# One strided sum for pooled values, a new order of the first loads, two joined chunks and a moved wait

## The chip, the cores and the metric

One core of a Trainium2 chip runs the whole program. The metric is the device time of one execution in microseconds (us). The engines are TensorE (PE in profile rows; PEld is its weight load), VectorE (DVE), ScalarE (ACT), GpSimd (POOL) and SyncE (SP, which issues most DMAs). Each runs its own instruction stream in order, and they wait for one another through semaphores.

## The reference, cut to what matters

An attention layer with pooled keys and values feeds a mixture of experts in which each token takes one expert.

```python
# 8 batches, 8 heads, 576 positions, 64 wide; pool = 8, so 72 pooled keys per head
k_p = k.reshape(B, H, Sp, pool, D).mean(axis=3)
v_p = v.reshape(B, H, Sp, pool, D).mean(axis=3)
attn = softmax(q @ k_p^T / sqrt(D))
x = (attn @ v_p)                      # as rows: 4608 tokens x 512
e_idx = argmax(x @ w_gate, axis=1)    # one of 8 experts per token
out[mask_e] = gate_w * eom * (relu(x @ w1[e]) @ w2[e])   # 512 -> 1024 -> 512
```

## The kernel before, in words

**Attention and routing** (up to about 150 us) goes over 36 tiles of 128 tokens; a batch is 4.5 tiles. Each tile has two halves `a` (heads 0 to 2 or so, and the rest), and the loop at the end of `attention_and_routing` writes out the order by hand: for tile `i` it issues the scores on TensorE, the row maxima (`peak`, VectorE, line 281), the exponentials (`softmax`, ScalarE), and, for older tiles, the transposes of the probabilities, the product with the values (`values`) and the division by the sum (`normalise`, VectorE, line 332, after a reciprocal, line 326). Other work is put between these: `at(step, f, ...)` calls `f` after a given half tile, and a queue of generators gives out pieces through `work(n)`, four pieces per half tile. All engines take their instructions in this written order, so an instruction that waits holds back all that is written behind it on its engine.

**Pooling.** Keys and values are loaded unpooled, eight rows to a pooled row. For batches 1 to 7 GpSimd adds keys in halves (`pool_k`, line 201) and makes the first halving of the values (`halve_v`, line 223, five chunks of 256 columns); VectorE makes the other two halvings (`pool_v`, line 227), for three chunks and then for two, as four queue pieces from `pooled(b)`. For batch 0 VectorE does everything: `ready_k(0)` and `first_v(0)` are written before the loop, `ready_k(1)` and `first_v(1)` after the first half tile, ahead of the second half's `peak`. The buffer of unpooled values, `vt`, is one for all batches: the next batch's load waits until it has been pooled.

**First loads.** SyncE issues, in this order: keys of the first four heads' half (576 KB), all values (1280 KB), the first tile's queries (256 KB), the other keys (576 KB), the other queries (896 KB).

**Tail.** `TAIL` is an order written out by hand for the end of routing and the start of the first expert's work: `M` is one of eight chunks of the first layer on TensorE (12 matmuls of 384 columns, four of them on the low part of the tokens), `H` and `L` round it to a high and a low part on ScalarE and VectorE, `a d A D` split weights into high and low parts, `W` gives out routing pieces, `T` loads the table of jobs into registers, and `Y` is a chunk of the second layer. After it every engine changes over to its own loop over the experts' jobs.

**Experts** (from about 175 us): TensorE alternates the first layer (line 1015) and the second (line 996); VectorE scales the result (line 1186) and GpSimd scatters it to the output by an indirect DMA (line 1328). At the end of each job GpSimd waits until its scatters have landed, and at the very end for its last gathers.

Of the kernel before, what the change touches and what calls it, by code (L numbers as in the profile page):

```python
# [15 lines left out]
AF = mybir.ActivationFunctionType  # L16
# [7 lines left out]
P = 128  # L24
# [33 lines left out]

TAIL = 'M W9 a H L W3 d M a H L W6 d M a H L W6 d M a H L W6 d A M H L W12 A D M H L A D R M H L A D T M D Y Y Y Y Y H L'.split()
F0 = TAIL.count('Y')

AHEAD = {3: 8, 2: 8, 1: 2}
# [26 lines left out]
def attention_and_routing(ctx, tc, sh, qT, kT, v, wg, wst, xs):  # L91
# [95 lines left out]
    def load_v(b):  # L187
        nc.sync.dma_start(vt, v[b].rearrange("p (c f) -> p c f", c=5))

    def load_first():  # L190
        k_t[0], q_t[0] = sh.k[0], sh.q[0]
        k, q = kT[0].rearrange("p (c r n) -> p c r n", r=POOL, c=4), qT[0].rearrange("p (c s) -> p c s", c=4)
        nc.sync.dma_start(k_t[0][:, 0:2], k[:, 0:2])
        load_v(0)
        nc.sync.dma_start(q_t[0][:, :, 0:P], q[:, :, 0:P])
        nc.sync.dma_start(k_t[0][:, 2:4], k[:, 2:4])
        nc.sync.dma_start(q_t[0][:, :, P:S], q[:, :, P:S])

    def pool_k(b, eng, w, c0, c1):
        k = k_t[b][:, c0:c1]  # L200
        eng.tensor_tensor(k[:, :, 0:w], k[:, :, 0:w], k[:, :, w:2 * w], op=ALU.add)  # L201

    def scale_k(b, c0=0, c1=4):
        for h in range(2):
            r = slice(64 * h, 64 * h + 64)
            nc.scalar.activation(kbd[b % 2][r, c0:c1, KEYS * h:KEYS * h + KEYS], k_t[b][r, c0:c1, 0], AF.Copy, scale=1.0 / 64)

    def ready_k(a):
        for w in (4, 2, 1):
            pool_k(0, nc.vector, w, 2 * a, 2 * a + 2)  # L210
        scale_k(0, 2 * a, 2 * a + 2)

    def pooled_rows(b):
# [9 lines left out]
            nc.gpsimd.tensor_tensor(vt[:, c, 0:256], vt[:, c, 0:256], vt[:, c, 256:512], op=ALU.add)  # L223

    def pool_v(b, a, n):
        to = vt[:, part_v(a), 0:n] if n > D else pooled_rows(b)[:, part_v(a)]
        nc.vector.tensor_tensor(to, vt[:, part_v(a), 0:n], vt[:, part_v(a), n:2 * n], op=ALU.add)

    def first_v(a):
        for n in (4 * D, 2 * D, D):  # L230
            pool_v(0, a, n)

    def place_v(b, c):
        t = vbd[b % 2]
# [36 lines left out]
    def scores(i, a):  # L271
        s = s_t[i, a] = sh.p_h[(2 * i + a) % 3]
        for c in range(2):
            for r0, n, b, s0 in segments(i):
                nc.tensor.matmul(s[r0:r0 + n, 144 * c:144 * c + 144], q_t[b][:, 2 * a + c, s0:s0 + n],  # L275
                                 kbd[b % 2][:, 2 * a + c, :], start=True, stop=True)

    def peak(i, a):
# [208 lines left out]

    def first_layer(kind):
        if kind == "M":
            f = len(layered)  # L490
            layered.append((sh.p_h + sh.p_y[1:])[f % 4][:, 0:WIDE * P])
            hidden_chunk(nc, sh, f, layered[f], f == 0)
        elif kind == "Y":
            outputs.append(output_chunk(nc, sh, len(outputs), sh.p_y[0], 0))
        elif kind == "a":
            split_hi(halves[0])
        elif kind == "d":
            split_lo(halves.pop(0))
        elif kind == "A":
            split_piece.append(len(split_piece))  # L500
            split_hi(2 * 4 + split_piece[-1], 1)
        elif kind == "D":
            split_lo(2 * 4 + split_done.pop(), 1)
        elif kind == "T":
            assert not queue
            for eng in (nc.tensor, nc.scalar, nc.vector, nc.gpsimd, nc.sync):
                sh.loaded[eng.engine] = nc.values_load_multi_w_load_instructions(
                    sh.table[0:1, 0:E + 2], [eng.engine], min_val=0, max_val=1023,
                    skip_runtime_bounds_check_because="counts of a few bits each")[1]
        elif kind == "R":  # L510
# [16 lines left out]

    def pooled(b):
        for a in range(2):
            for n in (2 * D, D):  # L530
                pool_v(b, a, n)
                yield 0

    tick = [0]

# [48 lines left out]
    prepare_buffers(2)  # L584
    prepare_counts()
    ready_k(0)
    first_v(0)
    at(-0.5, ready_k, 1)
    at(-0.5, first_v, 1)
    at(1.5, prepare_routing)  # L590
    at(3, no_rows, E)
    for e in range(E):
# [57 lines left out]
    return x.rearrange("p g f -> p (g f)"), x.rearrange("p g (d t) -> p d g t", d=4), halves  # L650


def hidden_chunk(nc, sh, f, acc, late):
    terms = [(d, part, x) for d in range(4) for part, x in ((0, 0), (0, 1), (1, 0))]
    if late:
        terms.sort(key=lambda term: term[2])
    for d, part, x in terms:
        o = DM * f + P * d
        i = nc.tensor.matmul(acc, sh.w1[0][:, part, o:o + P], sh.xt[:, x, d, :], start=((d, part, x) == terms[0]), stop=((d, part, x) == terms[-1]))
    return i  # L660


def output_chunk(nc, sh, f, acc, k):
# [64 lines left out]
def experts(st, nc, sh, wst, xs, out):  # L728
# [557 lines left out]
    @blk.gpsimd  # L1286
    def _(eng):
        copy = nc.gpsimd.tensor_copy

        def columns(u):  # L1290
            u = nc.s_assert_within(u, 0, R - WIDE, skip_runtime_bounds_check_because="there are at most 50 slots")
            return ids[:, bass.ds(u, WIDE)]

        def past(name, val):
            val = eng.to_reg(val)
            eng.wait_ge(q["on"], 1)
            eng.wait_ge(q[name], val)

        def take(u):
            copy(nx, xm[:, :, ID - DM:ID - DM + 2]).then_inc(q["c"], 1)  # L1300
            copy(src, columns(u)).then_inc(q["c"], 1)  # L1301

        def gather(sems):
            for k in range(WIDE):
                nc.gpsimd.indirect_dma_start(out=xm[:, k].bitcast(I32), out_offset=None, in_=xs,  # L1305
                                             in_offset=bass.IndirectOffsetOnAxis(ap=src[:, k:k + 1], axis=0)).then_inc(sems[k], 16)

        def ahead(u, job, more):
            if not isinstance(job, int):
                for k in range(WIDE):  # L1310
                    past(f"x{k}", 16 * job - 16)
            with eng.If(more > 0):
                take(u + 3)
            with eng.If(more <= 0):
                take(u + 2)
            past("c", 3 * job + 1)
            gather(X)

        def body(e, size, job, u, single, nth, more, last, late):
            past("y", u + 1)  # L1320
            copy(sc[:, 0:3:4 - size], nx[:, 0:size, 1]).then_inc(q["sc"], 1)
            copy(dst, nx[:, :, 0]).then_inc(q["c"], 1)
            past("sc", job + 1)
            past("c", 3 * job + 5)
            ahead(u + size, job + 2, more)
            for k in range(size):
                past("y", u + k + 2)
                nc.gpsimd.indirect_dma_start(out=out, out_offset=bass.IndirectOffsetOnAxis(ap=dst[:, k:k + 1], axis=0),  # L1328
                                             in_=yb[2 if k == size - 1 else k], in_offset=None, bounds_check=N - 1, oob_is_err=False).then_inc(q["out"], 16)
            past("out", 16 * (u + size))  # L1330

        eng.nop().then_inc(q["on"], 1)
        rows = table(eng)
        with eng.If(rows[E + 1] > 2):
            eng.nop().then_inc(q["c"], 2)
        with eng.If(rows[E + 1] <= 2):
            copy(src, columns(0)).then_inc(q["c"], 2)
            past("c", 2)
            gather([q["g"]] * WIDE)
            past("g", 16 * WIDE)  # L1340
        ahead(0, 1, rows[E + 1] & 1)
        eng.wait_ge(q["t"], ROWS)
        job, slot = loops(eng, rows, body)
        for k in range(WIDE):
            past(f"x{k}", 16 * job + 16)


def program():
# [54 lines left out]
def layout(q, k, v, moe_w_gate, moe_w_output_gate, moe_w1, moe_w2):  # L1403
# [2 lines left out]
    wg = np.zeros((2, D, 11, GATE), np.float32)  # L1406
    for a, slot, head in ((0, 0, 0), (0, 1, 1), (1, 2, 3), (1, 3, 4), (0, 4, 1), (0, 5, 2), (1, 6, 6), (1, 7, 7), (0, 8, 4), (0, 9, 5), (0, 10, 6)):
        wg[a, :, slot] = gates[head]
    rows = v.reshape(B, H, KEYS, POOL * D)
    vs = np.zeros((B, P, 5, POOL * D), np.float32)  # L1410
    for chunk, r0, head, k0, n in VROWS:
        vs[:, r0:r0 + n, chunk] = rows[:, head, k0:k0 + n]
    return {
        "qT": c(q.reshape(B, 4, 2, S, D).transpose(0, 2, 4, 1, 3)).reshape(B, P, 4 * S),
        "kT": c(k.reshape(B, 4, 2, KEYS, POOL, D).transpose(0, 2, 5, 1, 4, 3)).reshape(B, P, 4 * POOL * KEYS),
        "v": vs.reshape(B, P, 5 * POOL * D),
        "wg": wg.reshape(P, 11 * GATE),
# [10 lines left out]
```

## Time and profile before

| | us |
|---|---|
| median of 3 runs | 607.02 |
| lowest and highest of them | 606.26, 607.34 |
| the profiled execution's own time | 603.94 |
| its span, first to last instruction | 602.1 |
| TensorE busy in the span | 572.3 (95%) |
| VectorE busy | 365.1 (61%) |
| ScalarE busy | 257.8 (43%) |
| GpSimd busy | 223.1 (37%) |

The granted TensorE clock was 0.998 of full speed. Shares of busy time are means over two very different stages: attention up to about 150 us, the experts from about 175 us on. Instructions of one engine can overlap a little in the rows, so that busy times are slightly too high, those of TensorE above all.

### The profile page before, as it was taken

The numbers are of one execution on the slowest core, as the hardware profiler recorded it, in microseconds if no ns is written. First come the engines' busy times: TensorE is split into PE (matmuls) and PEld (weight loads), VectorE is DVE, ScalarE is ACT, GpSimd is POOL, SyncE is SP. The second block draws the span as 40 slices with busy tenths as digits, with TensorE's granted clock in tenths as the row PEclk, the third lists the DMA queues.
The fourth block names the chain that finished last, engine by engine and source line by source line (L and its number), as shares of the span: only waits on it lengthen the run. The fifth ranks groups of instructions, "written<-read, shape, count | busy, mean of one in ns | idle before, by whom it ended". The sixth has DMA issues, their size and how long they took to land.

```text
span 602.1 us, 11826 instructions
## 1 busy us (share of the span) xinstructions
PE 572.3 (95%) x3427; PEld 519.2 (86%) x3428; DVE 365.1 (61%) x892; ACT 257.8 (43%) x709; POOL 223.1 (37%) x331
## 2 busy tenths in 40 slices
PE   2999999999899999999999999999999999999996
PEld 2898898888888989898989898898988898989894
DVE  6789999988888625698575323664263842232323
ACT  2988998787435304266344120441141420302120
POOL 2858789642524322233234131231202421213131
PEclk9999999999999999999999999999999999999999
DMA  9856899966377433589666213463033212010111
GB/s 337 312 236 270 316 349 369 348 232 198 140 238 182 170 99 118 147 234 335 177 215 201 62 37 88 139 195 65 35 139 102 46 21 84 2 52 19 41 30 36
DMA packets 44684, 96.61 MB, mean 160 GB/s; under 512 B 5515, under 2 KB 28475, under 8 KB 41664
## 3 DMA queue, kind: packets, MB, share of 16 engines
q1 hardware_dynamic: 29328, 48.95, 25.3%
q10 hardware_dynamic: 7488, 27.27, 13.5%
q0 software_dynamic: 7792, 19.61, 9.3%
q14 instruction: 57, 0.47, 0.3%
q8 instruction: 19, 0.31, 0.2%
HBM read 76.36 MB, written 22.91 MB: 165 GB/s over the span
## 4 chain that ended last, share of the span: by engine, by line
PE 68%; issue 2%; DVEq 0%; DVE 0%; POOL 0%; POOLq 0%
PE p_h L1015 34%; PE p_y L996 33%; PE p_y L665 1%; POOL out L1328 0%; DVE rows L1186 0%; DVEq L1189 0%; PE p_y L1050 0%; DVE q_even L1212 0%; DVEq L779 0%; DVEq L780 0%; DVEq L1219 0%; DVEq L910 0%; DVEq L837 0%; DVEq L1211 0%; DVEq L860 0%
## 5 line engine op out<-in xcount | busy, mean ns | idle before, releaser
L1095 ACT ACTIVATE ht<-p_h 128x384 fp32r<-128x384 f32 (+1 forms) x104 | 46.9, 451 | 245.9 <-PE p_h L1015 243.7
L1015 PE MATMUL p_h<-xt,w1b 128*128 128x384 f32 (+1 forms) x736 | 115.5, 317 | 1.9 <-issue 1.3
L1015 PEld LDWEIGHTS p_h<-xt,w1b 128*128 128x128 f32 x736 | 114.4, 189 | 3.2 <-issue 2.8
L1328 POOL DMA_INDIRECT out<-rows,dst x41 | 43.1, 1051 | 199.8 <-DVE rows L1186 196.6
L1197 DVE SCALAR_TENSOR_TENSOR ht<-p_h,ht 128x384 fp32r<-128x384 f32 (+1 forms) x104 | 52.3, 504 | 98.4 <-ACT ht L1095 98.3
L996 PE MATMUL p_y<-w2b,ht 128*128 128x512 f32 x480 | 110.4, 390 | 0.0
L996 PEld LDWEIGHTS p_y<-w2b,ht 128*128 128x128 f32 x480 | 89.8, 188 | 18.4
L1015 PE MATMUL p_h<-xt,w1a 128*128 128x256 f32 (+1 forms) x640 | 93.7, 306 | 1.2 <-DVE q_even L1212 1.0
L1015 PEld LDWEIGHTS p_h<-xt,w1a 128*128 128x128 f32 x640 | 92.8, 190 | 2.3 <-DVE q_even L1212 1.2
L996 PE MATMUL p_y<-w2a,ht 128*128 128x512 f32 x408 | 94.2, 390 | 0.4 <-PE p_y L665 0.4
L996 PEld LDWEIGHTS p_y<-w2a,ht 128*128 128x128 f32 x408 | 76.2, 188 | 16.4 <-issue 0.9
L1186 DVE TENSOR_SCALAR rows<-p_y,sc 128x512 f32<-128x512 f32 x41 | 30.1, 741 | 85.9 <-PE p_y L996 71.5
L287 ACT ACTIVATE p<-p_h,m 128x72 f32<-128x72 f32 x288 | 69.9, 345 | 13.4 <-DVE m L281 13.0
L309 PE MATMUL p_y<-vbd,pT 128*128 128x162 f32 (+3 forms) x400 | 68.5, 320 | 3.8 <-DVE xg L332 2.6
L1305 POOL DMA_INDIRECT rows<-xs,src x51 | 56.0, 1099 | 24.9 <-POOL src L1301 13.4
L309 PEld LDWEIGHTS p_y<-vbd,pT 128*128 128x128 f32 (+1 forms) x400 | 54.2, 179 | 8.7 <-issue 2.5
L440 POOL DMA_INDIRECT xs<-xg,where x36 | 36.1, 1003 | 42.5 <-DVE grec L326 20.7
L201 POOL TENSOR_TENSOR kq<-kq 128x288 f32<-128x288 f32 (+1 forms) x63 | 40.8, 673 | 15.0 <-DMA kq<-kT 14.2
L275 PE MATMUL p_h<-kbd,q_even 128*128 128x144 f32 (+1 forms) x160 | 28.9, 308 | 11.6 <-DMA q_even<-qT 8.8
L332 DVE TENSOR_TENSOR xg<-p_y,grec 128x240 f32<-128x240 f32 x72 | 35.3, 490 | 1.3
L1150 DVE STREAM_TRANSPOSE turned<-rows 128x512 f32<-128x512 f32 x51 | 32.4, 686 | 4.0 <-DMA rows<-xs 2.2
L275 PEld LDWEIGHTS p_h<-kbd,q_even 128*128 128x128 f32 (+1 forms) x160 | 22.9, 191 | 13.7 <-issue 9.3
(170 smaller groups left out, 660.3 us busy)
## 6 DMA issues: line engine op xcount, KB each, us to landing
stage<-wst ACTq DMA_DIRECT2D x52, 512.0 KB, 4.7
rows<-v SPq DMA_DIRECT2D x8, 1280.0 KB, 6.3
kq<-kT SPq DMA_DIRECT2D x7, 1152.0 KB, 12.0
rows<-xs SPq DMA_DIRECT2D x36, 192.0 KB, 3.8
stage<-wst SPq DMA_DIRECT2D x12, 512.0 KB, 6.0
kq<-qT SPq DMA_DIRECT2D x4, 1152.0 KB, 9.5
q_even<-qT SPq DMA_DIRECT2D x3, 1152.0 KB, 8.8
rows<-xs SPq DMA_DIRECT2D x20, 128.0 KB
```

What stands on the lines that cost most here:

```text
L201: eng.tensor_tensor(k[:, :, 0:w], k[:, :, 0:w], k[:, :, w:2 * w], op=ALU.add)
L275: nc.tensor.matmul(s[r0:r0 + n, 144 * c:144 * c + 144], q_t[b][:, 2 * a + c, s0:s0 + n], kbd[b % 2][:, 2 * a + c, :], start=True, stop=True)
L287: nc.scalar.activation(pt[i % 3][:, o:o + KEYS], sv[:, h], AF.Exp, bias=m[:, h:h + 1])
L309: nc.tensor.matmul(av[r0:r0 + n, COLS * h:COLS * (h + n_heads)], pT[:, c, r0:r0 + n], vbd[b % 2][:, slot:slot + n_heads].rearrange("p h f ...
L332: nc.vector.tensor_tensor(xg[g][:, j, 0:LEAD + DM].rearrange("p (f h) -> p f h", h=H)[:, :, hs], avv[:, :, 0:GATE + D].rearrange("p h f -> ...
L440: ins = nc.gpsimd.indirect_dma_start(out=whole_rows(xs), out_offset=bass.IndirectOffsetOnAxis(ap=where, axis=0), in_=x.bitcast(I32), in_of ...
L996: i = mm(to, ht[:, h, f, P * k:P * k + P], w[:, part, o:o + DM], start=(f == 0 and part == 0 and h == 0), stop=(f == 7 and h == 1))
L1015: i = mm(to, w[:, part, o:o + P], x, start=(d == 0 and k == 0), stop=(d == 3 and k == len(terms) - 1))
L1095: act(ht[:, 0, f, 0:size * P], p_h[f % DEEP][:, 0:size * P], AF.Relu).then_inc(q["hh"], 1)
L1197: nc.vector.scalar_tensor_tensor(ht[:, 1, f, 0:n], src, 0.0, ht[:, 0, f, 0:n].bitcast(F32), op0=ALU.max, op1=ALU.subtract).then_inc(q["hl" ...
L1305: nc.gpsimd.indirect_dma_start(out=xm[:, k].bitcast(I32), out_offset=None, in_=xs, in_offset=bass.IndirectOffsetOnAxis(ap=src[:, k:k + 1], ...
L1328: nc.gpsimd.indirect_dma_start(out=out, out_offset=bass.IndirectOffsetOnAxis(ap=dst[:, k:k + 1], axis=0), in_=yb[2 if k == size - 1 else k ...
```

## The change

Four parts. VectorE's pooling becomes one `tensor_reduce` over a rearranged view, so that the summed index is innermost, with a step of 64 numbers (values) or 72 (the first batch's keys): 1536 and 1024 inputs per partition for batch 0's values, 768 and 512 for each later batch, 1152 for each half of batch 0's keys. Both reductions of batch 0's values are written after `ready_k(1)`, still ahead of the second half's `peak`; for later batches `pooled(b)` has two pieces instead of four. The first loads go in the order keys, queries, keys, queries, values, with batch 0's queries laid out so that each load has whole rows. In `TAIL` the first `M` computes chunks 0 and 1 together, the high part's matmuls of both before the low part's, and the other `M`s each move up by one place. GpSimd's wait for a job's scatters moves to the beginning of the next job, the last one behind the waits for the last gathers; the bound of the scatter's index sits in one register.

```diff
-TAIL = 'M W9 a H L W3 d M a H L W6 d M a H L W6 d M a H L W6 d A M H L W12 A D M H L A D R M H L A D T M D Y Y Y Y Y H L'.split()
+TAIL = 'M W9 a H L W3 d M a H L W6 d M a H L W6 d M a H L W6 d M A H L W12 A D M H L A D R M H L A D T D Y Y Y Y Y H L'.split()
...
     def load_first():
         k_t[0], q_t[0] = sh.k[0], sh.q[0]
-        k, q = kT[0].rearrange("p (c r n) -> p c r n", r=POOL, c=4), qT[0].rearrange("p (c s) -> p c s", c=4)
+        k = kT[0].rearrange("p (c r n) -> p c r n", r=POOL, c=4)
+        q0 = q_t[0].rearrange("p c s -> p (c s)")
         nc.sync.dma_start(k_t[0][:, 0:2], k[:, 0:2])
+        nc.sync.dma_start(q0[:, 0:4 * P], qT[0][:, 0:4 * P])
+        nc.sync.dma_start(k_t[0][:, 2:4], k[:, 2:4])
+        nc.sync.dma_start(q0[:, 4 * P:], qT[0][:, 4 * P:])
         load_v(0)
-        nc.sync.dma_start(q_t[0][:, :, 0:P], q[:, :, 0:P])
-        nc.sync.dma_start(k_t[0][:, 2:4], k[:, 2:4])
-        nc.sync.dma_start(q_t[0][:, :, P:S], q[:, :, P:S])
...
+    first_keys = sh.stage[0][:, 0:4 * KEYS].rearrange("p (c n) -> p c n", c=4)
...
     def ready_k(a):
-        for w in (4, 2, 1):
-            pool_k(0, nc.vector, w, 2 * a, 2 * a + 2)
+        c = slice(2 * a, 2 * a + 2)
+        nc.vector.tensor_reduce(first_keys[:, c], k_t[0][:, c].rearrange("p c r n -> p c n r"), axis=AX.X, op=ALU.add)
         scale_k(0, 2 * a, 2 * a + 2)
...
     def pool_v(b, a, n):
-        to = vt[:, part_v(a), 0:n] if n > D else pooled_rows(b)[:, part_v(a)]
-        nc.vector.tensor_tensor(to, vt[:, part_v(a), 0:n], vt[:, part_v(a), n:2 * n], op=ALU.add)
-
-    def first_v(a):
-        for n in (4 * D, 2 * D, D):
-            pool_v(0, a, n)
+        nc.vector.tensor_reduce(pooled_rows(b)[:, part_v(a)],
+                                vt[:, part_v(a), 0:n * D].rearrange("p c (r d) -> p c d r", r=n), axis=AX.X, op=ALU.add)
...
         if kind == "M":
-            f = len(layered)
-            layered.append((sh.p_h + sh.p_y[1:])[f % 4][:, 0:WIDE * P])
-            hidden_chunk(nc, sh, f, layered[f], f == 0)
+            accs = {}
+            for _ in range(1 if layered else 2):
+                f = len(layered)
+                accs[f] = (sh.p_h + sh.p_y[1:])[f % 4][:, 0:WIDE * P]
+                layered.append(accs[f])
+            hidden_chunks(nc, sh, accs)
...
     def pooled(b):
         for a in range(2):
-            for n in (2 * D, D):
-                pool_v(b, a, n)
-                yield 0
+            pool_v(b, a, POOL // 2)
+            yield 0
...
     ready_k(0)
-    first_v(0)
     at(-0.5, ready_k, 1)
-    at(-0.5, first_v, 1)
+    for a in range(2):
+        at(-0.5, pool_v, 0, a, POOL)
...
         def body(e, size, job, u, single, nth, more, last, late):
+            with eng.If(job > 0):
+                past("out", 16 * u)
             past("y", u + 1)
...
-            past("out", 16 * (u + size))
-
+        limit = eng.to_reg(N - 1)
...
         for k in range(WIDE):
             past(f"x{k}", 16 * job + 16)
+        past("out", 16 * slot)
```

`hidden_chunks` issues the same 12 matmuls per chunk as `hidden_chunk` did, sorted so that the high part's come first over both chunks. `scale_k` reads batch 0's pooled keys from `first_keys`, and `queries` finds batch 0's queries in their new layout.

## Rows read from the trace of the kernel before

**Rows 1.** The chain that ended last, in order of time: start us, us, what.
```profile
175.23 7.77 PE p_y L665 x33
...
598.09 1.00 POOL out L1328
```

**Rows 2.** Busy time by stretch: stretch, its us, busy us (instructions) of each engine, clock, DMA.
```profile
40.00:60.00 20.00, 19.27 (x155) 17.94 (x154) 18.17 (x67) 16.70 (x69) 14.17 (x19) 1.00 0.64 240
...
250.00:400.00 150.00, 149.84 (x866) 137.13 (x865) 91.83 (x134) 60.21 (x98) 44.24 (x56) 1.00 0.54 164
```

**Rows 3.** VectorE's timeline in a tile without pooling; brackets: idle before, and what ended it.
```profile
48.34 0.19 DVE L326 RECIPROCAL grec<-p_y 128x5 f32<-128x5 f32 x1 [0.77 <-PE p_y L309]
```

**Rows 4.** VectorE's groups from 21 to 150 us: busy us, mean ns | idle.
```profile
L227 DVE TENSOR_TENSOR rows<-rows 128x384 f32<-128x384 f32 x7 | 6.8, 976 | 1.7 <-POOL rows L223 1.7
...
L227 DVE TENSOR_TENSOR vp<-rows 128x192 f32<-128x192 f32 x7 | 3.8, 544 | 0.2
...
L227 DVE TENSOR_TENSOR rows<-rows 128x256 f32<-128x256 f32 x7 | 3.2, 464 | 0.0
...
L227 DVE TENSOR_TENSOR vp<-rows 128x128 f32<-128x128 f32 x7 | 2.1, 297 | 0.0
```

**Rows 5.** Single lines of VectorE: ns minimum/median/maximum, first and last start, shapes.
```profile
L687 DVE TENSOR_REDUCE rows<-rows x2: 328/913/1498, 169.8 to 177.8; 128x12 f32<-128x84 f32 x1, 128x100 f32<-128x700 f32 x1
...
L348 DVE TENSOR_REDUCE lg<-xg x9: 671/676/678, 35.9 to 153.9; 128x64 f32<-128x512 f32 x9
...
L360 DVE TENSOR_REDUCE best<-cand x9: 168/170/186, 37.7 to 155.3; 128x4 f32<-128x32 f32 x9
...
L354 DVE TENSOR_TENSOR d<-lg,mx x9: 181/245/1699, 36.8 to 154.9; 128x32 f32<-128x32 f32 x9
```

**Rows 6.** DMA issues by line: count, KB each, median us to landing.
```profile
rows<-v SPq DMA_DIRECT2D x8, 1280.0 KB, 6.3
...
kq<-kT SPq DMA_DIRECT2D x2, 576.0 KB, 5.7
...
q_even<-qT SPq DMA_DIRECT2D x1, 896.0 KB, 9.3
...
q_even<-qT SPq DMA_DIRECT2D x1, 256.0 KB, 7.0
```

**Rows 7.** The timeline of the first 27 us, all engines.
```profile
4.64 1.60 DVE L201 TENSOR_TENSOR kq<-kq 128x576 f32<-128x576 f32 x3 [0.47 <-DMA kq<-kT]
...
6.33 0.65 ACT L206 ACTIVATE kbd<-kq 64x144 f32<-64x144 f32 x2 [4.05 <-DVE kq L201]
...
7.86 1.55 DVE L227 TENSOR_TENSOR rows<-rows 128x768 f32<-128x768 f32 x2 [1.62 <-DMA rows<-v]
...
8.82 1.30 PE L275 MATMUL p_h<-kbd,q_even 128*128 128x144 f32 x4 [8.82 <-DMA q_even<-qT]
...
14.22 0.46 DVE L281 TENSOR_REDUCE m<-p_h 128x4 f32<-128x288 f32 x1 [0.71 <-PE p_h L275]
...
14.71 1.92 ACT L287 ACTIVATE p<-p_h,m 128x72 f32<-128x72 f32 x8 [1.91 <-DVE m L281]
...
23.41 1.07 DVE L227 TENSOR_TENSOR rows<-rows 128x384 f32<-128x384 f32 x1 [1.03 <-POOL rows L223]
```

**Rows 8.** The timeline from 150 to 176 us, all engines.
```profile
154.08 0.97 PE L659 MATMUL p_h<-xt,w1a 128*128 128x384 f32 x4 [0.61 <-DVE xt L483]
...
157.41 0.56 DVE L520 SCALAR_TENSOR_TENSOR ht<-p_h,ht 128x384 fp32r<-128x384 f32 x1 [1.14 <-ACT ht L516]
...
173.64 0.55 DVE L520 SCALAR_TENSOR_TENSOR ht<-p_y,ht 128x384 fp32r<-128x384 f32 x1
```

**Rows 9.** The last scatter of outputs and GpSimd's queue after it, from 585 us.
```profile
DMA to landing us min/median/max: 2.8/2.8/2.8
...
L1295 POOLq FUSED_REGOPS  x2: 161/178/196, 601.1 to 601.3; - x2
...
L1297 POOLq EVENT_SEMAPHORE  x5: 17/17/42, 591.9 to 601.7; - x5
```

More of the change, by code (lines that the diff above doesn't have):

```diff
@@ L191, in load_first, with queries @@
         k_t[0], q_t[0] = sh.k[0], sh.q[0]
-        k, q = kT[0].rearrange("p (c r n) -> p c r n", r=POOL, c=4), qT[0].rearrange("p (c s) -> p c s", c=4)
+        k = kT[0].rearrange("p (c r n) -> p c r n", r=POOL, c=4)
+        q0 = q_t[0].rearrange("p c s -> p (c s)")
         nc.sync.dma_start(k_t[0][:, 0:2], k[:, 0:2])
+        nc.sync.dma_start(q0[:, 0:4 * P], qT[0][:, 0:4 * P])
+        nc.sync.dma_start(k_t[0][:, 2:4], k[:, 2:4])
+        nc.sync.dma_start(q0[:, 4 * P:], qT[0][:, 4 * P:])
         load_v(0)
-        nc.sync.dma_start(q_t[0][:, :, 0:P], q[:, :, 0:P])
-        nc.sync.dma_start(k_t[0][:, 2:4], k[:, 2:4])
-        nc.sync.dma_start(q_t[0][:, :, P:S], q[:, :, P:S])
+    def queries(b, c, s0, n):
+        if b:
+            return q_t[b][:, c, s0:s0 + n]
+        q0 = q_t[0].rearrange("p c s -> p (c s)")
+        o, w, s = (0, P, 0) if s0 < P else (4 * P, S - P, P)
+        o += w * c + s0 - s
+        return q0[:, o:o + n]
     def pool_k(b, eng, w, c0, c1):
@@ L205, in scale_k @@
             r = slice(64 * h, 64 * h + 64)
-            nc.scalar.activation(kbd[b % 2][r, c0:c1, KEYS * h:KEYS * h + KEYS], k_t[b][r, c0:c1, 0], AF.Copy, scale=1.0 / 64)
+            pooled = k_t[b][r, c0:c1, 0] if b else first_keys[r, c0:c1]
+            nc.scalar.activation(kbd[b % 2][r, c0:c1, KEYS * h:KEYS * h + KEYS], pooled, AF.Copy, scale=1.0 / 64)
     def ready_k(a):
-        for w in (4, 2, 1):
-            pool_k(0, nc.vector, w, 2 * a, 2 * a + 2)
+        c = slice(2 * a, 2 * a + 2)
+        nc.vector.tensor_reduce(first_keys[:, c], k_t[0][:, c].rearrange("p c r n -> p c n r"), axis=AX.X, op=ALU.add)
         scale_k(0, 2 * a, 2 * a + 2)
@@ L274, in scores @@
             for r0, n, b, s0 in segments(i):
-                nc.tensor.matmul(s[r0:r0 + n, 144 * c:144 * c + 144], q_t[b][:, 2 * a + c, s0:s0 + n],
+                nc.tensor.matmul(s[r0:r0 + n, 144 * c:144 * c + 144], queries(b, 2 * a + c, s0, n),
                                  kbd[b % 2][:, 2 * a + c, :], start=True, stop=True)
@@ L650, in turned_rows, with hidden_chunks @@
     return x.rearrange("p g f -> p (g f)"), x.rearrange("p g (d t) -> p d g t", d=4), halves
[L653 to L657, printed above, removed]
+def hidden_chunks(nc, sh, accs):
+    terms = [(f, d, part, x) for f in accs for d in range(4) for part, x in ((0, 0), (0, 1), (1, 0))]
+    if 0 in accs:
+        terms.sort(key=lambda term: term[3])
+    seen = {f: 0 for f in accs}
+    for f, d, part, x in terms:
         o = DM * f + P * d
-        i = nc.tensor.matmul(acc, sh.w1[0][:, part, o:o + P], sh.xt[:, x, d, :], start=((d, part, x) == terms[0]), stop=((d, part, x) == terms[-1]))
-    return i
+        nc.tensor.matmul(accs[f], sh.w1[0][:, part, o:o + P], sh.xt[:, x, d, :], start=(seen[f] == 0), stop=(seen[f] == 11))
+        seen[f] += 1
 def output_chunk(nc, sh, f, acc, k):
@@ L1328, in body @@
                 nc.gpsimd.indirect_dma_start(out=out, out_offset=bass.IndirectOffsetOnAxis(ap=dst[:, k:k + 1], axis=0),
-                                             in_=yb[2 if k == size - 1 else k], in_offset=None, bounds_check=N - 1, oob_is_err=False).then_inc(q["out"], 16)
-            past("out", 16 * (u + size))
+                                             in_=yb[2 if k == size - 1 else k], in_offset=None, bounds_check=limit, oob_is_err=False).then_inc(q["out"], 16)
+        limit = eng.to_reg(N - 1)
         eng.nop().then_inc(q["on"], 1)
@@ L1408, in layout @@
         wg[a, :, slot] = gates[head]
+    qs = c(q.reshape(B, 4, 2, S, D).transpose(0, 2, 4, 1, 3)).reshape(B, P, 4 * S)
+    first = qs[0].reshape(P, 4, S)
+    qs[0] = np.concatenate([first[:, :, 0:P].reshape(P, 4 * P), first[:, :, P:].reshape(P, 4 * (S - P))], axis=1)
     rows = v.reshape(B, H, KEYS, POOL * D)
@@ L1413, in layout @@
     return {
-        "qT": c(q.reshape(B, 4, 2, S, D).transpose(0, 2, 4, 1, 3)).reshape(B, P, 4 * S),
+        "qT": qs,
         "kT": c(k.reshape(B, 4, 2, KEYS, POOL, D).transpose(0, 2, 5, 1, 4, 3)).reshape(B, P, 4 * POOL * KEYS),
```

## The prediction, made before the changed kernel was run

> **What bounds the kernel now.** I read the chain that ended last first. From 175.23 us on it is a chain of TensorE work down to the last scatter [rows 1], and the busy times by stretch agree: between 250 and 400 us TensorE is busy 149.84 of 150 us [rows 2]. Nothing in the change takes a matmul out of that stage, so time can come or go only before 175 us and after the last output. Before 150 us no engine is alone in front: between 40 and 60 us VectorE is busy 18.17 of 20 us, ScalarE 16.70, TensorE by its pipelined rows 19.27 [rows 2]. The reader is to see how this looks within a tile. Where VectorE has no pooling or routing to do, it waits 0.77 us for the product with the values [rows 3]: there the round of scores, exponentials and products sets the pace. Where pooling falls, its additions stand in VectorE's stream without idle time beyond the 1.7 us that the first ones wait for GpSimd's halves [rows 4]: there VectorE sets the pace, and a longer pooling makes the half tile longer.
>
> **What a strided sum costs.** The trace of before has two kinds of `tensor_reduce` from on-chip memory. With the summed index contiguous, 512 inputs took 676 ns and 32 took 170 (L348 and L360) [rows 5]: 1.05 ns an input and 0.14 us fixed. With the summed index at a step of 56 numbers, 84 inputs took 328 ns and 700 took 1498 (L687) [rows 5]: 1.90 ns an input and 0.17 us fixed. The change reads at steps of 64 and 72 numbers. These are the two bounds, and I take the second, since its access is the same in all but the length of the step:
> - half of the first keys, 1152 inputs: 2.36 us (lower bound 1.35), where the three additions took 1.60 [rows 7];
> - batch 0's values, 1536 and 1024: 3.09 and 2.11, together 5.2 us (lower bound 2.98);
> - each later batch, 768 and 512: 1.63 and 1.14, together 2.77 us (lower bound 1.62).
>
> The trace thus shows a price of nearly two for reading apart. The Trainium skill, SBUF — State Buffer, section "The DMA port swizzle", has a rule of that kind: memory lines of 16 bytes, with a penalty for each access that crosses to a new line. By that rule every input of these sums pays, and the sum is the one made below. The trace agrees (1.90 against 1.05).
>
> **Pooling of batches 1 to 7.** Removed: four additions a batch, with means of 976, 544, 464 and 297 ns, 2.28 us [rows 4]. These means hold time lost beside GpSimd: a small addition of 32 numbers varies from 181 to 1699 ns, while the reduction of 512 varies only from 671 to 678 [rows 5]. So I give the reductions no such loss. Added: 2.77 us. That is 0.49 us a batch, times seven 3.4 us longer. With the lower bound it would be 0.66 shorter, 4.6 in all; but in batches where VectorE waits for GpSimd's halves, a faster sum only waits longer, and I count half of it, 2.3. Both sums now stand ahead of the reciprocal and the division by the sum, which hold the bank that TensorE's next product with the values waits for; that is why I count the loss in full.
>
> **The start.** Keys reach the chip at 4.64 us, the values' 1280 KB at 7.86, queries at 8.82 [rows 6, 7]: some 400 KB a us. In the new order 256, 576, 896 and 1280 KB stand between the first keys and the end of the values, 3008 KB or 7.5 us, so values are there at about 12.2 us. VectorE: first keys 4.64 to 7.0; scaling takes 0.65 us, the scores 1.30, the maxima 0.46 [rows 7], so 9.6; second keys to 12.0; values from 12.2 to 17.4. Only behind these stands the second half tile's maximum, which started at 14.22 [rows 7]. So the queries' earlier arrival buys an earlier first score, and then VectorE stands 3.2 us later than before (0.9 with the lower bound: 12.2 and 2.98 make 15.1). ScalarE sat idle until that maximum and then began its exponentials [rows 7], so the delay passes on. One wait swallows part: at 23.41 VectorE had been idle 1.03 us for GpSimd's halves of batch 1 [rows 7]. GpSimd starts on them only after batch 1's keys, which do not move, and batch 1's values, whose load must now wait until 17.4 for the buffer and lands 6.3 us [rows 6] later at worst, 23.7; the first halves still come before the later VectorE wants them, or at most about as late. I take 3.2 less 1.03, 2.1 us (3.2 if nothing is swallowed, 0 with the lower bound).
>
> **The two joined chunks.** TensorE idled 0.61 us for the tokens' low part within the first chunk [rows 8]; eight more matmuls now fill this. But behind it VectorE is the one that works on: it waits 1.14 us for ScalarE at 157.41, and from there to 173.64 its rounding, splitting and table making follow each other without another wait [rows 8]. ScalarE's first rounding there waits for routing, not for the chunk. TensorE only reaches the changeover earlier and stands there. I count 0 and keep a gain of 0.6 as the bound; a chunk that VectorE waited for would be needed to earn it.
>
> **The moved wait.** The last scatter starts at 598.09 [rows 1] and lands 2.8 us after its issue [rows 9], at about 600.9. Then GpSimd still works on registers (161 and 196 ns from 601.1 on) and passes waits until 601.7 [rows 9]. Written before the last wait, this is done while the scatter is under way: 0.7 us less. The same wait at the start of a job stands where it stood, before the copies that free the output buffers; a branch more per job is covered by GpSimd's long waits for outputs. The index bound in a register saves at most hundredths.
>
> **The sum.** 3.4 for seven batches, 2.1 for the start, 0 for the chunks, less 0.7: 4.8 us, or 608.7 against the 603.94 of the profiled execution. The median of the runs shown, 607.02, stands 3.1 above that one, and I put the same 4.8 on it: 611.8.
>
> **Rivals.**
> - *The strided sum costs what a contiguous one does.* For it: the step differs from L687's, and seven inputs at a time are not four or eight. Against it: both sizes of L687 lie far off the contiguous line. Then 2.3 less for the batches, 0 for the start, 0.7 less at the end: 3.0 less, 604.0. It decides where a sum of 768 inputs takes less than about 1.3 us. The Trainium skill, VectorE: DVE Perf Modes, section on the perf-mode tiers, lists one rate for `tensor_reduce`, with no word on steps. By that rule this rival would hold; L687 speaks against it.
> - *The longer sums are hidden.* For it: the 0.77 us that VectorE waits in quiet tiles [rows 3]. If that slack takes up what the batches add and the start's delay is made good by half, 1.0 less 0.7 remains: 607.3. Against it: ScalarE and TensorE stop with VectorE in the half tile that pools, and have no spare pace to catch up.
> - *A step of 64 numbers costs more than one of 56.* At 3 ns an input, batches add 1.4 us each more and the start about 5, 15 in all: 627. No row speaks for it.
>
> **Chances and range.** My forecast 0.68, contiguous price 0.17, hidden 0.10, dearer step 0.05. The first alone gives 608.5 to 616, by the start's bound, by a loss that VectorE's waits partly soak up and by the spread between executions. From 603.8 to 616 the range leaves out about 2 in 10. What differs by less than 0.2%, 1.2 us, can hardly be told from no change here. Faster gets the contiguous price and a little of the hidden case, same most of the hidden case: 0.18, 0.11, slower 0.71.
>
> **What would show it.** In the new profile: the 128x192 sum from 768 inputs at about 1.63 us (0.95 would kill the forecast); the values' first sum starting near 12.2 us and the second half tile's maximum near 17.4; the attention's last tile and the changeover at 175.2 about 5.5 us later; TensorE without the 0.61 us gap in the first chunk but idle longer before the changeover; under 0.5 us between the last scatter's landing and the end. The forecast fails if the changeover comes earlier than before, or if the stretches in which an engine waits for nothing that the profile shows come out otherwise in the shifted code, which I can't price.

## The result and the profile after

The changed kernel took 612.03 us (median of 5 executions, 610.82 to 613.41); the kernel before took 607.02 beside it (606.26 to 608.09). The ratio is 1.0081 with a 95% interval of [1.0059, 1.0103], so the change costs 0.6% to 1.0%. The forecast was 611.8. Here and below a ratio leaves out executions more than 1.5% above the fastest of the same kernel, while a median takes all of them. The profiled execution's own time is 612.03, its span 610.2.

The chain that ended last, kernel after (start us, us, what), against [rows 1]:

```profile
182.21 9.38 PE p_y L676 x33
...
607.05 0.91 POOL out L1341
```

The changeover to the experts comes at 182.21 instead of 175.23, 6.98 us later. The 33 matmuls behind it take 9.38 us instead of 7.77. The windows on both sides of the changeover show why (stretch, its us, busy us of PE, PEld, DVE, ACT and POOL with instructions, clock, DMA share, GB/s):

```profile
175.86:182.21 6.35, 3.87 (x16) 2.57 (x16) 5.12 (x14) 0.49 (x1) 0.00 (x0) 1.00 0.54 182
182.21:191.60 9.39, 9.37 (x33) 7.22 (x33) 6.92 (x12) 2.00 (x2) 5.41 (x7) 0.82 0.78 201
```

TensorE stands for 2.5 of the last 6.35 us ahead of the changeover (in before it was busy for 5.36 of them), and the clock granted behind it is 0.82, between the two levels of 1.2 and 2.4 GHz. That is 1.6 us which the prediction did not have.

The timeline of the first 30 us, kernel after, against [rows 7]:

```profile
4.63 2.21 DVE L222 TENSOR_REDUCE stage<-kq 128x144 f32<-128x1152 f32 x1 [0.46 <-DMA kq<-kT]
...
7.69 1.30 PE L283 MATMUL p_h<-kbd,q_even 128*128 128x144 f32 x4 [7.69 <-ACT kbd L218]
...
9.40 2.20 DVE L222 TENSOR_REDUCE stage<-kq 128x144 f32<-128x1152 f32 x1
...
12.81 4.56 DVE L238 TENSOR_REDUCE vp<-rows 128x192 f32<-128x1536 f32 x2 [1.22 <-DMA rows<-v]
...
17.29 0.81 DVE L289 TENSOR_REDUCE m<-p_h 128x4 f32<-128x288 f32 x2
...
17.77 1.80 ACT L295 ACTIVATE p<-p_h,m 128x72 f32<-128x72 f32 x8 [5.49 <-DVE m L289]
...
23.03 3.47 POOL L235 TENSOR_TENSOR rows<-rows 128x256 f32<-128x256 f32 x5 [1.43 <-DMA rows<-v]
...
25.93 2.46 DVE L238 TENSOR_REDUCE vp<-rows 128x192 f32<-128x768 f32 x2
```

The first scores come 1.13 us earlier (8.82 to 7.69), for their queries are there; then VectorE waits 1.22 us for the values, and the second half tile's maximum starts at 17.29 instead of 14.22. ScalarE waits 5.49 us for it. VectorE's sums of batch 1 start at 25.93 instead of 23.41, and no longer wait for GpSimd.

VectorE's groups by shape, kernel after (busy us, mean ns | idle before), against [rows 4, 5]:

```profile
L238 DVE TENSOR_REDUCE vp<-rows 128x192 f32<-128x768 f32 x7 | 10.5, 1499 | 0.2 <-POOL rows L235 0.2
...
L238 DVE TENSOR_REDUCE vp<-rows 128x128 f32<-128x512 f32 x7 | 7.3, 1036 | 0.0
...
L238 DVE TENSOR_REDUCE vp<-rows 128x192 f32<-128x1536 f32 x1 | 2.8, 2755 | 1.2 <-DMA rows<-v 1.2
L238 DVE TENSOR_REDUCE vp<-rows 128x128 f32<-128x1024 f32 x1 | 1.9, 1887 | 0.0
```

From 768 to 1536 inputs the time grows by 1256 ns, 1.64 ns an input; from 512 to 768 by 463, 1.81. The forecast went by 1.90 and put the two sums of a batch at 1.63 and 1.14 us; they took 1.50 and 1.04.

The timeline from 155 to 185 us, kernel after, against [rows 8]:

```profile
158.82 4.45 PE L670 MATMUL p_h<-xt,w1a 128*128 128x384 f32 x24 [0.21 <-ACT xt L489]
...
182.21 3.21 PE L676 MATMUL p_y<-w2a,ht 128*128 128x512 f32 x9 [1.81 <-PEq L1407]
```

```profile
164.46 0.56 DVE L531 SCALAR_TENSOR_TENSOR ht<-p_h,ht 128x384 fp32r<-128x384 f32 x1 [1.14 <-ACT ht L527]
...
180.67 0.55 DVE L531 SCALAR_TENSOR_TENSOR ht<-p_y,ht 128x384 fp32r<-128x384 f32 x1
```

The joined chunks are one block of 24 matmuls without the 0.61 us gap. On VectorE nothing is won: its wait for ScalarE is 1.14 us as before, and both rows stand 7.05 and 7.03 us later than their counterparts in [rows 8].

Last, the timeline at the end, kernel after, against [rows 9]:

```profile
606.95 1.01 POOL L1341 DMA_INDIRECT out<-rows,dst  x1 [4.30 <-DVE rows L1197]
```

From the last scatter's start to the end of the span it is 610.2 less 606.95, 3.25 us, where it was 602.1 less 598.09, 4.01: 0.76 less. With the landing 2.8 us after the scatter as in [rows 9], 0.45 us are left to the end; under 0.5 was forecast.

### The profile page after: what moved, and what is told of

It reads as the page before. It is cut to its first block, busy times and chain, and to the rows that moved or that the text cites. A ratio compares the mean times of both kernels' runs of the same rounds, so it can differ in the third digit from the quotient of the medians.

```text
span 610.2 us, 11842 instructions
## 1 busy us (share of the span) xinstructions
PE 576.4 (94%) x3427; PEld 522.1 (86%) x3428; DVE 371.7 (61%) x870; ACT 256.8 (42%) x709; POOL 217.0 (36%) x331
## 4 chain that ended last, share of the span: by engine, by line
PE 66%; issue 2%; DVE 1%; DVEq 1%; ACT 0%; POOL 0%; POOLq 0%
PE p_h L1026 33%; PE p_y L1007 31%; PE p_y L676 2%; ACT w2b L1095 0%; DVE q_even L1223 0%; POOL out L1341 0%; DVE rows L1197 0%; DVE ht L1208 0%; DVE xt L1157 0%; DVEq L1200 0%; DVEq L1156 0%; ACT ht L1114 0%; DVEq L790 0%; DVEq L791 0%; DVE w2b L1185 0%
## 5 line engine op out<-in xcount | busy, mean ns | idle before, releaser
L1341 POOL DMA_INDIRECT out<-rows,dst x41 | 41.6, 1016 | 215.6 <-DVE rows L1197 213.1
L289 DVE TENSOR_REDUCE m<-p_h 128x4 f32<-128x288 f32 x72 | 32.3, 449 | 5.2 <-PE p_h L283 4.7
## 6 DMA issues: line engine op xcount, KB each, us to landing
kq<-kT SPq DMA_DIRECT2D x7, 1152.0 KB, 12.2
```

## The experiments

Twelve kernels ran, in three groups, each group on one chip: nine versions and three repeats. All compute the whole reference. Times are medians of 12 executions (one for the three repeats). The kernel before took 608.02, 608.01 and 608.07 us beside the three groups.

**The four parts alone.** *sums_only* has the strided sums in the old order of loads:

```diff
-        nc.vector.tensor_tensor(to, vt[:, part_v(a), 0:n], vt[:, part_v(a), n:2 * n], op=ALU.add)
+        nc.vector.tensor_reduce(pooled_rows(b)[:, part_v(a)],
+                                vt[:, part_v(a), 0:n * D].rearrange("p c (r d) -> p c d r", r=n), axis=AX.X, op=ALU.add)
```

> The kernel before with the strided sums alone (values and first keys), loads, chunks and waits as before. Theory A (the sums are the main loss): the sums of batches 1 to 7 take 1.50 and 1.04 us as in the changed kernel, batches add between 1.8 us (the sums' own time against the additions') and 4.3 us (what the reciprocals of tiles 1 and 28 shifted by in the changed kernel, 2.7 to 7.0), the start 0 to 0.9 (second half tile's maximum at about 15.1 instead of 14.22, mostly swallowed by the wait for GpSimd's halves): 608.8 to 612. Theory B (the late values are the main loss, the sums cost little): not over 1 us above before, 608 or less.

Measured: 610.03, ratio 1.0018 [0.9983, 1.0053]; changeover at 180.95. The median lies in theory A's range, but the interval does not leave out 1, so the time alone does not decide.

*order_only* has the new order of loads, with the additions of before:

```diff
         nc.sync.dma_start(k_t[0][:, 0:2], k[:, 0:2])
+        nc.sync.dma_start(q0[:, 0:4 * P], qT[0][:, 0:4 * P])
+        nc.sync.dma_start(k_t[0][:, 2:4], k[:, 2:4])
+        nc.sync.dma_start(q0[:, 4 * P:], qT[0][:, 4 * P:])
         load_v(0)
...
     ready_k(0)
-    first_v(0)
     at(-0.5, ready_k, 1)
-    at(-0.5, first_v, 1)
+    for a in range(2):
+        at(-0.5, first_v, a)
```

> The kernel before with the new order of the first loads alone, values summed by additions as before but behind the second keys, as in the change. Theory A: values land at 12.8, additions take 1.9 and 1.4 us, the second half tile's maximum starts at about 16.1 (+1.9), of which 1.0 is swallowed by the wait for GpSimd's halves: 607.5 to 609. Theory B (the late values are the main loss): the start's delay passes on in full and a little more, +2.5 to +3: 609.5 to 610.

Measured: 608.88, ratio 1.0013 [0.9982, 1.0044]; changeover at 179.76. The median is in theory A's range; the second half tile's maximum started at 15.62, 1.4 us later than in before, not 1.9. The interval does not leave out 1 here either.

*join_only* has the two joined chunks and the shifted `TAIL`:

```diff
-            hidden_chunk(nc, sh, f, layered[f], f == 0)
+            hidden_chunks(nc, sh, accs)
```

> The kernel before with the two joined chunks alone. Theory A: VectorE carries the tail, so the changeover stays at 175.2 within 0.3 us; TensorE stands idle longer ahead of it, and if that is what lowered the granted clock behind it in the changed kernel (0.82 for 9.4 us), the 33 matmuls behind the changeover take 9.4 us instead of 7.8 again: 607.0 to 608.7. Rival (the filled gap pays): changeover 0.6 to 1.4 earlier and no lowered clock, 605.6 to 606.4.

Measured: 610.23, ratio 1.0044 [1.0006, 1.0082]; changeover at 177.78, and the clock behind it fell. So the lowered clock came as theory A had it, while the changeover, which it had at 175.2 within 0.3 us, did not. Busy times ahead of it and behind it, *join_only*, columns as above:

```profile
171.43:177.78 6.35, 3.84 (x17) 2.54 (x15) 5.10 (x14) 0.49 (x1) 0.00 (x0) 1.00 0.58 188
177.78:187.18 9.40, 9.39 (x33) 7.21 (x33) 6.63 (x12) 2.00 (x2) 5.65 (x7) 0.82 0.79 201
```

*wait_only* has the moved wait:

```diff
         def body(e, size, job, u, single, nth, more, last, late):
+            with eng.If(job > 0):
+                past("out", 16 * u)
...
-            past("out", 16 * (u + size))
...
+        past("out", 16 * slot)
```

> The kernel before with the moved wait and the bound in a register alone. Theory A: only the end changes, the span ends 3.25 us instead of 4.01 after the last scatter's start, 0.75 us less: 606.3. Rival (the branch that each job gains on GpSimd delays its copies, which free the output buffers): no gain or a loss, 607 or more.

Measured: 606.68, ratio 1.0000 [0.9964, 1.0036]. The last scatter, timeline of *wait_only* (span 605.0):

```profile
601.79 1.00 POOL L1330 DMA_INDIRECT out<-rows,dst  x1 [4.32 <-DVE rows L1186]
```

It starts 3.21 us before the end of the span, 0.80 less than in before. The total of one kernel scatters by several us, so no median here can show 0.8; the row can.

**A ruler for the attention.** None of the four intervals but that of *join_only* leaves out 1. So I read the traces by tile: the start of each tile's reciprocal on VectorE (the row of [rows 3] in another tile), less its start in the first profile of before. As an instance, tile 19 in before, in the repeat of before, in *wait_only* and in after:

```profile
92.24 0.17 DVE L326 RECIPROCAL grec<-p_y 128x3 f32<-128x3 f32 x1
```

```profile
92.41 0.16 DVE L326 RECIPROCAL grec<-p_y 128x3 f32<-128x3 f32 x1
```

```profile
92.26 0.17 DVE L326 RECIPROCAL grec<-p_y 128x3 f32<-128x3 f32 x1
```

```profile
98.03 0.17 DVE L334 RECIPROCAL grec<-p_y 128x3 f32<-128x3 f32 x1
```

The table gives this difference in us for all profiles used, with the changeover's difference and time at the right; the kernels from *no_join* on, but for after, are told further down.

| profile | tile 4 | tile 13 | tile 19 | changeover | at us |
|---|---|---|---|---|---|
| before again | +0.16 | +0.14 | +0.17 | +1.39 | 176.62 |
| wait_only | +0.26 | +0.06 | +0.02 | +3.79 | 179.02 |
| join_only | +0.05 | +0.03 | +0.08 | +2.55 | 177.78 |
| join_again | +0.17 | +0.14 | +0.10 | +3.02 | 178.25 |
| order_only | +1.35 | +1.40 | +1.45 | +4.53 | 179.76 |
| sums_only | +0.56 | +0.91 | +3.66 | +5.72 | 180.95 |
| no_join | +1.54 | +1.92 | +4.62 | +6.23 | 181.46 |
| after | +2.92 | +3.06 | +5.79 | +6.98 | 182.21 |
| after_again | +2.38 | +3.07 | +6.62 | +8.57 | 183.80 |
| contiguous | −0.33 | −1.62 | −0.05 | +1.61 | 176.84 |
| contig_no_join | +0.11 | −0.98 | +0.01 | +3.83 | 179.06 |
| contig_old_order | +1.10 | −0.07 | +0.94 | +3.83 | 179.06 |

Five profiles (the first of before and the first four of the table) run the same attention code. From tile 4 to tile 19 they agree within 0.3 us. Behind it, between about 93 and 130 us, they drift apart by up to 3.8 us. So up to tile 19 a difference of half a us from them is not chance of the old code. The changed attention code scatters more: *no_join*, after and after_again run it alike, and lie 1.4 us apart at tile 4 and 2.0 at tile 19. They differ from the start, where the values' first sum began at 12.11, 12.81 and 12.28. So for the changed code what is lost between two tiles says more than how late one tile is. At the changeover a single profile tells little; the mean of the five is 177.4, and the first profile of before, against which the forecast was made, was the quickest.

The repeat of before was run to see that:

> The kernel before once more, for another profile. Four other kernels with the same code between tiles 19 and 25 lost about 2.5 us there against the first profile of before, and its own time, 603.94, was under every timed run. Theory A: that profiled execution was a quick one, and this one shows the same 2.5 us between tiles 19 and 25, span about 604.5 to 605. Rival: it repeats the first profile, span 602.

Measured: 605.02, changeover at 176.62, span 603.2: in between. Between tiles 19 and 25 it lost 0.8 us, not 2.5.

**The step of the sum.** *contiguous* is the changed kernel with values and first keys laid out in memory so that the summed rows lie next to each other (batch 0's values in two runs of four rows); the count of inputs and the order of the work stay.

```diff
-                                vt[:, part_v(a), 0:n * D].rearrange("p c (r d) -> p c d r", r=n), axis=AX.X, op=ALU.add)
+                                (vt[:, part_v(a), 0:n * D].rearrange("p c (d r) -> p c d r", r=n) if n < POOL else
+                                 vt[:, part_v(a)].rearrange("p c (h d r) -> p c d h r", h=2, r=4)),
+                                axis=AX.X if n < POOL else AX.XY, op=ALU.add)
```

> The changed kernel with the values laid out by the host so that the four rows which VectorE sums lie next to each other, and batch 0's keys with the eight rows next to each other: the same sums with the same number of inputs, in the same places. Theory A (the step costs): 768 and 512 inputs take 0.95 and 0.68 us instead of 1.50 and 1.04, batch 0's 1.76 and 1.22, its keys 1.35; the second half tile's maximum starts near 15.8 instead of 17.3, the batches give back about 3, the changeover comes 3 to 5 us earlier, 607.5 to 609. Rival (a sum costs its inputs, however they lie): durations and time as in the changed kernel, 612.

Measured: 607.93, ratio to before 0.9999 [0.9969, 1.0030]. VectorE's groups by shape, *contiguous*:

```profile
L238 DVE TENSOR_REDUCE vp<-rows 128x192 f32<-128x768 f32 x7 | 6.6, 944 | 0.4 <-POOL rows L235 0.2
...
L238 DVE TENSOR_REDUCE vp<-rows 128x128 f32<-128x512 f32 x7 | 4.8, 681 | 1.3 <-POOL rows L235 1.2
...
L238 DVE TENSOR_REDUCE vp<-rows 128x192 f32<-128x1536 f32 x1 | 1.8, 1753 | 2.1 <-DMA rows<-v 2.1
L238 DVE TENSOR_REDUCE vp<-rows 128x128 f32<-128x1024 f32 x1 | 1.2, 1209 | 0.0
```

The same counts cost 944 and 681 ns instead of 1499 and 1036. So the step makes the price, and all of the changed kernel's loss up to tile 19 is gone (+4.62, +5.79 and +6.62 become −0.05). The time is in theory A's range, 607.5 to 609. The start, timeline of *contiguous*:

```profile
12.04 2.88 DVE L238 TENSOR_REDUCE vp<-rows 128x192 f32<-128x1536 f32 x2 [2.12 <-DMA rows<-v]
14.83 0.81 DVE L291 TENSOR_REDUCE m<-p_h 128x4 f32<-128x288 f32 x2
```

The second half tile's maximum starts at 14.83, where the prediction's lower bound (12.2 and 2.98) gave 15.1.

**The joined chunks.** *no_join* is the changed kernel with the old `TAIL` and `hidden_chunk`.

> The changed kernel with the chunks and their order put back as before; sums, loads and wait as changed. Theory A (joining leaves TensorE idle ahead of the changeover, and the clock granted behind it is lower for that): the changeover stays near 182 us, the 33 matmuls behind it take 7.8 us instead of 9.4, and the time falls by about 1.6 us, to 610.4. Rival (the lowered clock has nothing to do with the join): 9.4 us again, 612.

Measured: 610.86, ratio to before 1.0070 [1.0048, 1.0091]. The 33 matmuls took 7.76 us, as theory A had it.

*join_more_y* is before with the joined chunks and seven instead of five `Y` ahead of the changeover (the cut is against *join_only*):

```diff
-... A D T D Y Y Y Y Y H L
+... A D T D Y Y Y Y Y Y Y H L
```

> The kernel before with the joined chunks and seven instead of five chunks of the second layer written ahead of the changeover, so that TensorE has work in the time that the join frees. Theory A: the changeover stays where it is, 27 matmuls are left behind it (6.4 us at full clock instead of 7.8), and with less idle time the clock stays up: 1.4 less than before, 606.6 against 608.0 for before on the same chips. Rival (the clock falls because the join packs the matmuls, not because TensorE idles): 27 matmuls at a lower clock, 7.7 us, 608.

Measured: 608.28, ratio 1.0026 [0.9991, 1.0060]. Its profiled execution was its longest (615.67), with a lower clock elsewhere. In it the 27 matmuls took 6.40 us, as theory A had it, but the median lies nearer to the rival's 608, so neither is borne out.

*join_again* and *after_again* profile two kernels a second time:

> The joined chunks alone, profiled again. If the join itself makes the clock fall behind the changeover, the 33 matmuls take 9.4 us again and not 7.77. Rival: it was chance in that execution, and they take 7.77.

> The changed kernel, profiled again. If the joined chunks make the clock fall behind the changeover whenever TensorE has idled long enough ahead of it, the 33 matmuls take 9.4 us again. Rival: chance, 7.77 us, and the whole execution about 1.6 us shorter than the first one.

Measured: 607.28 and 612.24. The same windows around the changeover, *join_again*:

```profile
171.90:178.25 6.35, 3.85 (x17) 2.55 (x15) 5.09 (x14) 0.49 (x1) 0.00 (x0) 1.00 0.56 191
178.25:187.65 9.40, 8.96 (x38) 7.11 (x39) 6.31 (x11) 2.01 (x2) 5.65 (x7) 1.00 0.81 201
```

TensorE stood as long ahead of the changeover as in *join_only* (3.85 us busy and 3.84), and the clock stayed at 1.00. In *after_again* the clock stayed at 1.00 as well, and the 33 matmuls took 7.75 us; yet the execution was no shorter, since its changeover came 1.6 us later. So the clock fell in two of the six profiles with the joined chunks and in none of the eight without. My theory, that the join makes it fall whenever TensorE has idled ahead, is refuted; that the join makes it likelier is possible and not shown.

**Towards a faster version.** *contig_old_order* is before with the moved wait and the sums laid out as in *contiguous*; *contig_no_join* is *contiguous* with the old `TAIL`.

> The kernel before with the moved wait and with the one sum over values laid out so that the summed rows lie next to each other; old order of the first loads, no joined chunks. If the price of a sum without a step is the one that the laid-out version showed (944 and 681 ns a batch against 2.28 us of additions), seven batches give back 0.66 us each at most, half of it where VectorE only waits longer for GpSimd, so 2.3 to 4.6 us, and the wait 0.7: 3 to 5 us below the kernel before, 603 to 605. Rival: what VectorE saves in a pooling tile is lost again in its waits for GpSimd, and the moved wait alone remains: 607.3.

> The changed kernel with the laid-out values and keys, and without the joined chunks; against it the laid-out version with the join (607.93). If the join costs by a lower granted clock behind the changeover in some executions, this version lies 0.5 to 1.5 us lower, 606.4 to 607.4, and its 33 matmuls there take 7.76 us. Rival: the laid-out version never had the lower clock (its profile shows 7.76 us too), so the join costs nothing in it: 607.9.

Measured: 606.61, ratio to before 0.9977 [0.9947, 1.0008], and 606.76, ratio 0.9956 [0.9926, 0.9985]. The second is the only version whose interval lies below 1, but the two medians are alike, so it is not shown to be the faster of the two. *contig_old_order* missed its 603 to 605. *contig_no_join* came out at 606.4 to 607.4 as expected, with 7.77 us for the 33 matmuls; since *contiguous* with the join took 7.76 in its profile, this does not show that the clock parts the two. Both won less than 3 us: what the cheap sum saves on VectorE does not come out at tile 19 (+0.94 and +0.01).

**Where it goes.** Between the first reciprocals of tiles 16 and 17 VectorE has no pooling at all. All seven profiles with additions take 3.60 to 3.65 us there, all seven with the one sum, strided or laid out, 5.18 to 5.62. In six of the seven it is two steps of the routing on 32 numbers that take longer, here the second of them in before and in *sums_only*:

```profile
82.68 0.65 DVE L366 TENSOR_TENSOR zs<-lg,oh 128x32 f32<-128x32 f32 x1
```

```profile
85.25 1.70 DVE L368 TENSOR_TENSOR zs<-lg,oh 128x32 f32<-128x32 f32 x1
```

The first one, `d`, goes from 0.24 to 0.80; together this is 1.6 us. In *contiguous* `d` (1.48) and `oh` (1.81 instead of 0.51) take longer. `d` is the operation that the prediction saw vary from 181 to 1699 ns. GpSimd's work differs there: in *sums_only* it adds keys from 85.34 to 86.28 us and again from 86.40 to 88.19, in before from 82.77 to 83.71 and, after a scatter of tokens, from 85.04. That this is the cause was not tried by itself.

## Why the prediction was right

**The total** was forecast 4.8 us up and came out 5.0 up. It is made of the changeover and the end. At the changeover the two profiles of after (182.21 and 183.80, mean 183.0) lie 5.6 us behind the mean of the five that run the old attention code (177.4); the forecast was 3.4 and 2.1, 5.5. The end gave back 0.76 where 0.7 was forecast. 5.6 less 0.76 is about 4.9. The two profiles of after against the first of before alone would have given 7.8, a figure that the timed runs do not bear out. That the total is met so closely is in part luck, as the batches below show.

**The price of a strided sum** was the right one of the two, 7% to 12% too high: 1499 and 1036 ns against 1.63 and 1.14 us, 2755 against 3.09, 2202 against 2.36. The lower bounds (0.95, 0.68, 1.76) are what *contiguous* took, within 10 ns. The 16-byte rule of the Trainium skill, SBUF — State Buffer, section "The DMA port swizzle", asks for a penalty of this sign. The one rate that the Trainium skill, VectorE: DVE Perf Modes, section on the perf-mode tiers, gives for `tensor_reduce` does not hold across these layouts: 1499 against 944 ns for 768 inputs.

**The start** was forecast 3.2 us late at the second half tile's maximum, and it was 3.07 late (17.29); in after_again and *no_join* it started at 16.77 and 16.60. The values' first sum was put near 12.2 and started at 12.81, in the other two at 12.28 and 12.11. The wait for GpSimd ahead of batch 1's sums was to swallow about 1 us, and in after that wait is gone (25.93). What remains is read at tile 4, behind batch 1's sums: forecast 2.1 and 0.49, 2.6; the three kernels with that start have +1.54, +2.92 and +2.38, mean 2.3. Neither part alone makes it: the sums alone leave +0.56 and the new order alone +1.35, 1.9 together. The three kernels scatter by 1.4 us, so the mean bears out the term but not its size to a few tenths.

**The batches** are the term that was mis-sized: 0.49 us each, over seven batches 3.4. Between tile 4 and tile 19 VectorE sums batches 2 to 5; the forecast there is 2.0. *sums_only*, *no_join*, after and after_again lost 3.1, 3.1, 2.9 and 4.2 us, about 0.8 a batch. From tile 19 to the changeover, with batches 6 and 7 and a forecast of 1.0, they lost 2.1, 1.6, 1.2 and 2.0; but the five with the old code lost 0 to 3.8, mean 2.1, so nothing there can be put on the sums. The two errors cancel, and that is luck: 1.3 us too little from tile 4 to tile 19, and 1.0 behind it that does not stand out from the old code's drift. By their own durations the sums cost 2.54 us a batch against 2.28 of the additions, 0.25 more; the rest of the 0.8 is not in the instruction. The forecast took out the additions with their means (976 ns for the first of them, which took between 0.54 and 1.76 us) and gave the sums no lost time. Of the 3.1 us that *sums_only* lost between tile 4 and tile 19, 1.6 came between tiles 16 and 17, where no sum stands and small routing steps take longer; so lost time did not simply leave with the additions. The laid-out sums point the same way: they take 1.62 us a batch, 0.66 less than the additions, and yet *contig_no_join* and *contig_old_order* change by only −0.1 and −0.2 us over the four batches. In both layouts a batch costs half a us or more beyond the sums' durations (0.8 less 0.25, and 0 less −0.66). Over the four batches 1.6 us of it, most of it, are those routing steps. Why they take longer, and what the rest is, stays open; that both sums now stand as one block ahead of the reciprocal and the division, as the forecast argued, was not tried by itself.

**The rival of the contiguous price** would therefore have failed in its own number too: it gave 3.0 us less than before, and *contiguous*, which has that price, is at 0.9999 of before.

**The joined chunks** were priced at 0 with a gain of 0.6 as the bound. On VectorE's chain that holds: the wait of 1.14 us stayed and nothing came earlier. But the bound may lie on the wrong side. In all three pairs the version with the join is the slower one: *join_only* 1.0044 against 1, the changed kernel 1.0081 against 1.0070 without it, *contiguous* 0.9999 against 0.9956 without it. That is 0.1% to 0.4%, 0.7 to 2.7 us, and only the first interval by itself leaves out no change. Of the other two pairs the intervals overlap and the halves ran in different groups, so that the join costs is not shown. One way in which it could cost is seen in two profiles, the clock behind the changeover, 1.6 us each time. The forecast had TensorE "stand there" at no price; it should have kept a loss as a bound. How often that happens, and whether the join brings it about, stays open. With this and the batches' two errors the total is closer than its terms.

**The moved wait** was forecast at 0.7 and gave 0.76 in after and 0.80 alone. The same wait at the beginning of a job and the branch cost nothing that shows: *wait_only* is at 1.0000.

**The hidden case and the dearer step** fell: the tiles did not soak up the loss up to tile 19, and no sum took 3 ns an input.

## What to carry to other kernels

A sum over a strided axis is one instruction, but here each input cost 1.6 to 1.8 ns instead of 1.05; look for a row of the same access before giving up additions for it, or lay the data out so that the summed axis is contiguous. The time that a mean holds beyond the quickest case need not go with the operation that is removed: here other small operations took 1.6 us longer in a stretch without any pooling. Before a forecast is set against one profile, compare the moment of its changeover with that of another execution of the same kernel: here the same code came there at 175.2 to 179.0 us, while from tile 4 to tile 19 it agreed within 0.3. An earlier load helps only if what it overtakes is not needed soon: the first scores came 1.1 us earlier, and the later values with the longer sums held back the second half tile by 2.4 to 3.1.

## What the runs showed of the hardware

**Executions differ by their clock.** Over the three groups, 87 executions of before ran with a mean granted clock from 0.983 to 1.000. The 39 with 0.996 or more had a median of 606.9 us, the other 48 one of 610.1. Of *join_only* 10 of 12 lay below 0.996 (median 610.85; the other two 607.0), of *sums_only* none. Sorted like this the join costs nothing at the higher clock, though two executions are few. So some of what a median shows is how often an execution loses clock. Of *contiguous* and of *contig_no_join* 10 of 12 lay below 0.996 too, although their medians are the lower ones.

**Where it was lost in one of them**, *contig_no_join*, windows within the attention:

```profile
95.00:100.00 5.00, 3.83 (x30) 3.56 (x29) 4.93 (x13) 4.26 (x18) 4.89 (x10) 1.00 0.98 385
100.00:104.00 4.00, 3.14 (x16) 2.79 (x17) 3.54 (x17) 2.79 (x13) 1.92 (x3) 0.68 1.01 423
104.00:108.00 4.00, 4.00 (x19) 3.06 (x20) 1.74 (x11) 2.21 (x10) 1.34 (x2) 0.50 0.28 112
```

TensorE stood for 1.2 of the first 5 us, then the clock went down to 0.50, the lower of its two levels, for 4 us. This is the stretch behind tile 19, where the unchanged executions also drift apart. In *wait_only*, though, TensorE stood as long in the first nine of these 13 us (2.0 us in both) and kept 1.00:

```profile
95.00:100.00 5.00, 3.99 (x28) 3.36 (x26) 4.68 (x10) 3.63 (x16) 4.80 (x9) 1.00 0.97 387
100.00:104.00 4.00, 3.00 (x21) 2.51 (x22) 3.97 (x18) 2.90 (x14) 3.45 (x6) 1.00 1.00 419
```

There the DMA engines are busy nearly all the time, VectorE too. What makes the unchanged executions drift there was not settled. One part of it is clock: between 117 and 122 us *wait_only* had 0.66 where before had 1.00, and from tile 25 to tile 28 it lost 1.4 us more.
